# Attention with a recurrent state: TensorE's instructions in slots of a fixed order

## The chip, the cores and the metric

The kernel runs on one core of a Trainium2 chip. The time is that of the device for one execution, in microseconds, as the median of several runs. The engines are TensorE (PE, with its weight loads PEld), VectorE (DVE), ScalarE (ACT), GpSimd (POOL) and SyncE (SP, whose queue issues nearly all DMAs). Each engine takes its instructions strictly in the order in which the compiler queued them.

## The reference

Attention keeps a 40 x 40 state for each of 4 x 8 heads and walks 768 steps; a mixture of eight experts follows, of which every token takes two.

```python
for t in range(S):                                    # S = 768, state [B, H, 40, 40]
    y[:, :, t] = np.einsum('bhd,bhde->bhe', rt, state)
    Sa = np.einsum('bhde,bhe->bhd', state, at)
    state_decay = state * wt[:, :, None, :] - np.einsum('bhd,bhe->bhde', Sa, bt)
    state = state_decay + np.einsum('bhd,bhe->bhde', vt, kt)
x = y.transpose(0, 2, 1, 3).reshape(B * S, H * D)      # 3072 x 320
logits = x @ w_gate
noisy_logits = logits + np.log1p(np.exp(x @ w_noise)) * noise
# the two best of 8 experts per token, softmax over the two, then
out[mask] += top2_w[mask, k, None] * (np.maximum(x[mask] @ w1[e], 0.0) @ w2[e])
```

## The kernel before, in words

*Units.* The 768 steps are cut into 12 chunks of 64, the four batches into two pairs p. A unit n is one chunk of one pair (24 units, n = 2 cc + p), with 8 heads x 2 batches in it. Four units in a row (two chunks of both pairs) make a group g of six.

*Preparation of a group.* `prepA` loads w, b and a, takes running products of w (DVE), logarithm and exponential (ACT), products (DVE, POOL), splits b and a into two 16-bit halves (`pack`), sends them through DRAM and loads them back as `st_ab` in the layout for TensorE (five such buffers, `SAB=5`). `scoresL` multiplies b with a for each chunk and copies the result into `lt` and `lo`, which go through DRAM into the tile X; `tsolve` inverts the triangular 32 x 32 blocks of X in 60 instructions, on DVE for group 0 and on POOL for the others (L552, L553); the result returns through DRAM (`fetchB`) as `dT`, one buffer for each pair. `prepC` does for k what `prepA` does for b and a.

*A unit.* `pre` multiplies k with a (`psc`, masked to `ak`) and starts W with ak times v. `chain` adds the state times a to W, splits W into two halves (`split320`, L609 on ACT and L610 on DVE), applies dT to get Q (`apply`, 24 matmuls), copies it (L646), corrects the lower half of W by it, splits again, applies dT again to get U, copies U three times (L653 to L655) and forms the next state S of its pair. `state` splits the state and stacks it, `turned` transposes it. `outp` transposes U, forms scores with r for both batches (`psc`, masked to P, L676), sums the output Y, and multiplies it by the gate `pgm` into xt (L687). `blocks` transposes k and b into `kb`. `logits` stores xt, transposes it and multiplies by the gate's weights; after tiles 8, 16, 20, 22 and 24 `route` picks the experts, counts places with matmuls (`pr`, L137 to L140) and leaves indirect DMAs on POOL that scatter the entries (L162), which are held back until the last `tsolve` is issued.

*Order.* A scheduler at compile time queues each engine's instructions by a simulated time, by priority where several are ready: the chain is raised by `PRIO`. `burst` chains the matmuls of one tile, so that they stay together; between bursts the scheduler is free. `ND=(2,0,0,0)` puts two matmuls without use ahead of Q (`warm`). The loop over units is in `run` (L721 to L741): `prepA` of a later group is issued `LA=7` units ahead, `prepC` `LC=4`, `fetchA` and `fetchB` two units ahead. PSUM has eight banks: one `psc`, one `pst`, three `pacc` (W, Q, U, S, Y), two `pt`, one `pp`.

*After attention* `experts` loads the weights of each expert, gathers its rows and multiplies; it isn't touched.

Of the kernel before, what the change touches and what calls it, by code (L numbers as in the profile page):

```python
# [21 lines left out]
NA=20  # L22
# [3 lines left out]
SG=1  # L26
# [15 lines left out]
class Moe:  # L42
    def __init__(s,nc,tc,ctx,aps):
        s.nc,s.tc=nc,tc
        s.wgn_d,s.nz_d,s.w1_d,s.w2_d,s.out_d=aps
        ec=ctx.enter_context
        s.kp=ec(tc.tile_pool(name="mk",bufs=1))
        s.rp=ec(tc.tile_pool(name="mr",bufs=MRB))
        s.dp=ec(tc.tile_pool(name="md",bufs=1,space=DRAM))
        s.scat=[]; s.half=0; s.parts=PARTS; s.cap=CAP; s.rts=list(RTS); s.todo=[]; s.sg=None  # L50
        s.consts()
# [50 lines left out]
    def logits(s,n,xt,ps,tag,bufs=(1,1)):  # L102

        nc=s.nc
        s.xw=nc.sync.dma_start(s.xd[n>=NA][128*n:128*n+128],xt)
        px=ps.tile([128,3,128],F32,name="px",tag=tag[0],bufs=bufs[0])
# [3 lines left out]
        pl=ps.tile([128,16],F32,name="pl",tag=tag[1],bufs=bufs[1])  # L110
# [16 lines left out]
    def route(s,n0,T,ps,tag,bufs):  # L127
# [7 lines left out]
        cnt=r("cnt",dt=F16); nc.vector.tensor_tensor(cnt,oh[:,:,0],oh[:,:,1],op=ALU.add)  # L135
        pr=ps.tile([128,T,8],F32,name="pr",tag=tag,bufs=bufs)
        nc.tensor.matmul(pr,s.tri,cnt,start=True,stop=False,skip_group_check=True)  # L137
        nc.tensor.matmul(pr,s.ones,s.cumh.rearrange("p (o e)->p o e",o=1).to_broadcast([128,T,8]),start=False,stop=False,skip_group_check=True)
        for j in range(T-1):
            nc.tensor.matmul(pr[:,j+1:],s.ones,cnt[:,j:j+1].to_broadcast([128,T-1-j,8]),start=False,stop=j==T-2,skip_group_check=True)  # L140
# [244 lines left out]
class Att:  # L385
    PSC=1; PACC=3; PT=2; PPB=1
    def __init__(s,nc,tc,ctx,aps):
# [9 lines left out]
        s.psa=ec(tc.tile_pool(name="psa",bufs=1,space=PSUM)); s.psb=ec(tc.tile_pool(name="psb",bufs=1,space=PSUM)); s.ps=ec(tc.tile_pool(name="ps",bufs=1,space=PSUM))  # L397
        s.consts()
    def consts(s):
# [7 lines left out]
        m=s.wk.tile([128,128],F32,name="mfull",tag="ak"); nc.gpsimd.memset(m,IS)  # L407
# [17 lines left out]
        s.tri=t([128,32,32],F16,name="tri"); nc.gpsimd.memset(s.tri,1.0)  # L425
        nc.gpsimd.affine_select(out=s.tri,in_=s.tri,pattern=[[-1,32],[1,32]],base=0,channel_multiplier=0,compare_op=ALU.is_gt,fill=0.0)
# [41 lines left out]
    def prepA(s,p,g):  # L468
# [26 lines left out]
        gm=s.tmp.tile([120,2,3,CG],F32,name="gm")  # L495
# [35 lines left out]
    def scoresL(s,G,gi,scr):  # L531

        nc=s.nc
        lt=s.tmp.tile([128,CG,8,32],F32,name="lt",bufs=LTB)
        lo=s.tmp.tile([128,CG,8,32],F32,name="lo",bufs=LOB)
        for c in range(CG):
            pp=s.score64(G['b'][c],G['a'][c],"pp",s.PPB)
            for z,t0 in ((lt,0),(lo,32)): nc.scalar.activation(z[:,c],pp[:,:,t0:t0+32],AF.Copy,scale=-(2.0**-18))
        for i in range(4):
            s.sl=s.nc.sync.dma_start(scr[gi,i].rearrange("c h (j t)->j (c h) t",j=32),(lt,lo)[i%2][32*i:32*i+32].rearrange("p c h t->p (c h) t"))  # L540
        G['lo']=lo
    def tsolve(s,scr,eng):
# [3 lines left out]
        eng.tensor_tensor(Xt,Xt,s.tri,op=ALU.mult)  # L546
# [8 lines left out]
        nc.scalar.activation(th[...,0],Xt,AF.Copy,scale=SC)  # L555
        nc.vector.scalar_tensor_tensor(th[...,1],Xt,SC,th[...,0],op0=ALU.mult,op1=ALU.subtract)
# [4 lines left out]
    def fetchA(s,G,cc,c,n):  # L561
        nc=s.nc; o={'n':n,'G':G,'c':c}; p=G['p']
# [6 lines left out]
        rv=s.RV[n%2]  # L569
        for j in range(2): nc.sync.dma_start(rv[64*j:64*j+48,j:j+2].rearrange("p x i b t->p (x i b t)"),s.aps[3][p,cc,j])  # L570
# [8 lines left out]
    def warm(s,src,k):  # L579
        if not k: return  # L580
        for _ in range(k): s.nc.tensor.matmul(src,s.idh,s.dm[:,0:320],start=True,stop=True)
# [107 lines left out]
    def run(s,m,xo=None):  # L689
# [3 lines left out]
        def prepA(g,p):  # L693
            if p==0: grp[g]=[]; scr[g]=s.dr.tile([2,4,CG,8,1024],F32,name="scr")
# [198 lines left out]
```

## Time and profile before

| what | us |
|---|---|
| three runs | 1025.58, 1022.32, 1024.23 |
| median | 1024.23 |
| the profiled execution | 1027.86 |
| its span, first to last instruction | 1026.1 |
| busy in the span: PE, PEld | 793.2, 704.1 |
| busy: DVE, ACT, POOL | 512.5, 397.6, 475.2 |

The span has four parts: preparation of the first group until 99 us, attention until about 580, the change-over to the experts until 606, and the experts. A row of a group of instructions names the line, engine, operation, tile written and tiles read, shapes and number; then busy us, mean ns of one, and the idle time of the engine just before with what ended it. A row in order of time begins with its start in us and its duration.

### The profile page before, as it was taken

The numbers are of one execution on the slowest core, as the hardware profiler recorded it, in microseconds if no ns is written. First come the engines' busy times: TensorE is split into PE (matmuls) and PEld (weight loads), VectorE is DVE, ScalarE is ACT, GpSimd is POOL, SyncE is SP. The second block draws the span as 40 slices with busy tenths as digits, with TensorE's granted clock in tenths as the row PEclk, the third lists the DMA queues.
The fourth block names the chain that finished last, engine by engine and source line by source line (L and its number), as shares of the span: only waits on it lengthen the run. The fifth ranks groups of instructions, "written<-read, shape, count | busy, mean of one in ns | idle before, by whom it ended". The sixth has DMA issues, their size and how long they took to land.

```text
span 1026.1 us, 25154 instructions
## 1 busy us (share of the span) xinstructions
PE 793.2 (77%) x10506; PEld 704.1 (69%) x10506; DVE 512.5 (50%) x1023; ACT 397.6 (39%) x816; POOL 475.2 (46%) x616
## 2 busy tenths in 40 slices
PE   0111557729687787998799569999999999999995
PEld 0111446518575676877688449999999989999995
DVE  9359874443566446447355542644344434443430
ACT  2202343423353344455454322544344434343421
POOL 6201347968347818827875235133333333333313
PEclk9999975868687677899899669999999999999998
DMA  3794998393579358666265753526252525252303
GB/s 96 190 202 125 231 247 216 87 257 100 141 195 249 95 125 204 160 142 179 76 129 138 241 166 61 136 49 149 49 149 49 148 50 147 51 147 51 36 7 39
DMA packets 135264, 136.20 MB, mean 133 GB/s; under 512 B 67393, under 2 KB 114949, under 8 KB 135061
## 3 DMA queue, kind: packets, MB, share of 16 engines
q1 hardware_dynamic: 123492, 117.35, 43.1%
q0 software_dynamic: 11648, 17.15, 9.5%
q8 instruction: 85, 1.39, 0.6%
q14 instruction: 39, 0.31, 0.1%
HBM read 96.48 MB, written 41.37 MB: 134 GB/s over the span
## 4 chain that ended last, share of the span: by engine, by line
PE 46%; POOL 16%; DMA 14%; DVE 10%; issue 8%; ACT 3%; SPq 2%; POOLq 0%; ACTq 0%; DVEq 0%
PE po L295 16%; PE ph L273 13%; POOL X L553 6%; POOL Tt L552 5%; PE pY L452 3%; DMA X<-scr 3%; PE psc L452 2%; PE pW L452 2%; PE pt L254 2%; DMA d_ab<-pk 2%; DMA rawk<-in_fm_dram 2%; DMA out_dram<-y,le 2%; DMA xr<-xd,le 1%; PE pQ L452 1%; POOL X L546 1%
## 5 line engine op out<-in xcount | busy, mean ns | idle before, releaser
L297 POOL DMA_INDIRECT out_dram<-y,le x56 | 92.5, 1652 | 201.3 <-ACT y L296 172.1
L276 DVE SCALAR_TENSOR_TENSOR hl<-ph,hh 128x256 fp32r<-128x256 f32 (+1 forms) x128 | 71.0, 557 | 154.7 <-ACT hh L274 154.3
L274 ACT ACTIVATE hh<-ph 128x320 fp32r<-128x320 f32 (+1 forms) x128 | 66.2, 519 | 156.6 <-PE ph L273 156.5
L553 POOL TENSOR_TENSOR X<-X,Tt 128x30 f32<-128x30 f32 (+9 forms) x150 | 86.6, 577 | 10.6
L241 POOL DMA_INDIRECT xr<-xd,le x56 | 54.3, 970 | 74.3 <-DMA le<-ls 33.0
L552 POOL TENSOR_TENSOR Tt<-X 128x30 f32<-128x30 f32 (+9 forms) x150 | 82.0, 547 | 10.0
L295 PE MATMUL po<-w2h,hh 128*128 128x320 f32 x384 | 74.6, 314 | 0.0
L273 PE MATMUL ph<-xh,w1h 128*128 128x512 f32 (+1 forms) x256 | 71.3, 362 | 0.5 <-ACT xh L257 0.5
L273 PE MATMUL ph<-xh,w1l 128*128 128x512 f32 (+1 forms) x256 | 69.7, 354 | 0.0
L273 PE MATMUL ph<-xl,w1h 128*128 128x512 f32 (+1 forms) x256 | 69.0, 351 | 0.0
L295 PE MATMUL po<-w2l,hh 128*128 128x320 f32 x384 | 68.3, 312 | 0.0
L295 PE MATMUL po<-w2h,hl 128*128 128x320 f32 x384 | 68.1, 309 | 0.0
L452 PEld LDWEIGHTS <-st_ab 120*64 120x64 f16 (+1 forms) x928 | 28.6, 123 | 51.7 <-issue 41.8
L295 PEld LDWEIGHTS po<-w2h,hh 128*128 128x128 f32 x384 | 61.3, 188 | 3.1
L452 PE MATMUL psc<-RV,uT 128*64 128x128 f32 x384 | 59.9, 306 | 4.2 <-DVE P L676 3.9
L676 DVE TENSOR_TENSOR P<-psc,mk 128x512 f32<-128x512 f32 x48 | 33.0, 688 | 56.2 <-PE psc L452 55.8
L452 PEld LDWEIGHTS <-dT 128*128 128x128 f16 x1152 | 39.8, 102 | 29.4 <-issue 14.8
L452 PE MATMUL psc<-RV 128*64 128x128 f32 x384 | 60.0, 306 | 0.0
L295 PEld LDWEIGHTS po<-w2h,hl 128*128 128x128 f32 x384 | 59.3, 188 | 0.1
L295 PEld LDWEIGHTS po<-w2l,hh 128*128 128x128 f32 x384 | 58.9, 188 | 0.4
L452 PE MATMUL pQ<-w,dT 128*128 128x40 f16 x1152 | 42.1, 187 | 21.6 <-DMA dT<-scr 10.0
L162 POOL DMA_INDIRECT ls<-ent,po x48 | 47.4, 988 | 19.3 <-issue 14.1
(299 smaller groups left out, 1939.2 us busy)
## 6 DMA issues: line engine op xcount, KB each, us to landing
w2r<-in_w_dram SPq DMA_DIRECT2D x8, 1280.0 KB
RV<-in_rv_dram SPq DMA_DIRECT2D x48, 192.0 KB
rawba<-in_fm_dram SPq DMA_DIRECT2D x24, 360.0 KB
d_ab<-pk SPq DMA_DIRECT2D x24, 360.0 KB
st_ab<-d_ab SPq DMA_DIRECT2D x36, 240.0 KB
w1r<-in_w_dram SPq DMA_DIRECT2D x8, 1024.0 KB
raww<-in_fm_dram SPq DMA_DIRECT2D x12, 365.6 KB
st_ab<-d_ab SPq DMA_DIRECT2D x24, 180.0 KB
```

The source lines that it names most:

```text
L162: st=nc.gpsimd.indirect_dma_start(out=s.ls[s.half],out_offset=OFFS(ap=po[:,j,k:k+1],axis=0),in_=s.ent[:,j,k],in_offset=None)
L241: for k in range(c,c+a): nc.gpsimd.indirect_dma_start(out=x[:p,k],out_offset=None,in_=s.xd[w],in_offset=OFFS(ap=li[:p,k,0:1],axis=0))
L254: for t,p in tiles(t0,n): nc.tensor.transpose(pt[:,t-t0:t-t0+p],x[:p,t//128,f0:f0+128],s.idm[:p,:p])
L273: for i,(a,b) in enumerate(mm): nc.tensor.matmul(ph[:,:n],a,b,start=i==0,stop=i==7)
L274: nc.scalar.activation(hh[:,f,:n],ph[:,:n],AF.Relu)
L276: if c.stop>c.start: nc.vector.scalar_tensor_tensor(o,ph[:,c],0.0,hh[:,f,c].bitcast(F32),op0=ALU.max,op1=ALU.subtract)
L295: nc.tensor.matmul(po[:p],h[:,f,r],w[:,f],start=k==0,stop=k==23); k+=1
L297: st=nc.gpsimd.indirect_dma_start(out=s.out_d,out_offset=OFFS(ap=idx[:p,ii],axis=0),in_=y[:p],in_offset=None,compute_op=ALU.add)
L452: def mm(s,*a,**k): return lambda: s.nc.tensor.matmul(*a,**k)
L552: eng.tensor_tensor(t,Xt[:,j:j+1,j+1:].to_broadcast([128,j,m]),Xt[:,0:j,j:j+1].to_broadcast([128,j,m]),op=ALU.mult)
L553: s.tl=eng.tensor_tensor(Xt[:,0:j,j+1:],Xt[:,0:j,j+1:],t,op=ALU.add)
L676: nc.vector.tensor_tensor(m,pp.rearrange("p i j t->p (i j) t"),s.mk.to_broadcast([128,8,64]),op=ALU.mult)
```

## The change

`burst` now chains each matmul or transpose of attention to the one before it in the program, whatever tile it is of, and the route's matmuls go through it too: PE's order is the order in which the program is written. `chain`, `pre` and `outp` are cut into steps, and `slot(n)` writes them out: unit n's chain with steps of the output of n-1, of the keys and the state of n+1, of the logits of n-2, and of the scores of a group in between. Two more buffers for the turned state, one more for kb; ak has one. `psc` has two banks, which the state's stacking and the group scores share. `route` is cut in two, its matmuls come a slot later. X is masked by a select instead of a product, and the constant for it is gone. The matmuls without use are gone. `LA` is 8, the loads of r and v (`fetchR`) are issued after those of k and v of the next but one unit.

```diff
-            s.route(s.n0,s.rts.pop(0),ps,tag[1],bufs[1])
+        if j==s.rts[0]-1: s.pend=s.route1(s.n0,s.rts.pop(0)); s.n0=n+1
+    def places(s,ps,tag,bufs):
+        if s.pend is None: return
+        n0,T=s.pend[:2]; n=n0+T-1
+        s.route2(*s.pend,ps,tag,bufs); s.pend=None
...
     def burst(s,f):
-        last=None
         for g in f:
-            with (s.tc.high_priority(offset=BURST) if last is not None else ExitStack()): i=g()
-            if last is not None: s.tc.add_manual_dep(i.ins,last.ins.name,...)
-            last=i
+            i=g()
+            if s.pel is not None: s.tc.add_manual_dep(i.ins,s.pel.ins.name,...)
+            s.pel=i
...
-    PSC=1; PACC=3; PT=2; PPB=1
+    PSC=2; PACC=3; PT=2; PPB=1
...
-            pp=s.score64(G['b'][c],G['a'][c],"pp",s.PPB)
+        pp=s.score64(G['b'][c],G['a'][c],"psc",s.PSC)
...
-        eng.tensor_tensor(Xt,Xt,s.tri,op=ALU.mult)
+        nc.gpsimd.affine_select(out=Xt,in_=Xt,pattern=[[-1,32],[1,32]],base=0,channel_multiplier=0,compare_op=ALU.is_gt,fill=0.0)
...
-        nc.scalar.activation(th[...,0],Xt,AF.Copy,scale=SC)
-        nc.vector.scalar_tensor_tensor(th[...,1],Xt,SC,th[...,0],op0=ALU.mult,op1=ALU.subtract)
+        for r in (slice(0,16),slice(16,32)):
+            nc.scalar.activation(th[:,r,:,0],Xt[:,r],AF.Copy,scale=SC)
+            nc.vector.scalar_tensor_tensor(th[:,r,:,1],Xt[:,r],SC,th[:,r,:,0],op0=ALU.mult,op1=ALU.subtract)
...
-            pe=s.psa.tile([120,8,40],F32,name="pst",tag="pst",bufs=1)
+            pe=s.psa.tile([120,8,40],F32,name="pst",tag="psc",bufs=s.PSC)
...
-        sD=s.wk.tile([128,4,2,40],F32,name="sD",bufs=1)
+        sD=s.wk.tile([128,4,2,40],F32,name="sD",bufs=3)
...
+    def slot(s,n,O,x,m,sc):
+        o,oP,oN=O.get(n),O.get(n-1),O.get(n+1)
+        if o:
+            if not first: s.burst([s.mm(W[...],o['a'](h,b),o['sE'][:,b,h],...) for h,b in HB()])
+            w1=s.split320("w1",W,IS)
+        if oP: s.scores(oP,0)
+        if sc: s.scoresL(*sc,0)
+        if n-2 in x: x[n-2]['xT']=m.turned(x[n-2]['xt'],s.ps,"pt",s.PT)
+        if sc: s.scoresL(*sc,1)
+        if o:
+            Q=...; s.apply(Q,dT,pr(w1,0),pr(w1,1),True,True)
+            q=...; nc.scalar.activation(q,Q,AF.Copy)
+        if oN:
+            s.keys(oN)
+            if oN['cc']: oN['sD']=s.turned(oN['G']['p'])
+        if o:
+            s.burst([s.mm(W[...],o['lo'][r(b),h],q[r(b),h],...) for h,b in HB()])
+            w2=s.split320("w1",W,IS)
+        if oP: s.scores(oP,1); s.gates(oP)
+        if o:
+            U=...; s.apply(U,dT,pr(w2,0),pr(w2,1),True,True)
+            (three copies of U as before)
+        if oN and oN['cc']: oN['sE']=s.estack(oN['G']['p'])
+        m.places(s.ps,"pp",s.PPB)
+        if n-2 in x: m.logits(n-2,x[n-2]['xT'],s.ps,"pp",s.PPB)
+        if o and not last:
+            (S as before, from the split state and U, into Sst)
+            s.split(p)
+        if o: s.uturned(o)
+        if oN: s.blocks(oN)
+        if oP:
+            s.outp(oP); x[n-1]={'xt':oP['xt'][:,0:DM]}
+            m.put(n-1,x[n-1]['xt'])
+        if sc: s.gamma(sc[0])
+        if oN: s.sums(oN)
...
+        sc={1:(1,0),2:(1,1)}
+        for g in range(2,NG): n=max(4*g-LS,3); sc[n]=(g,0); sc[n+1]=(g,1)
+        for n in range(N+3):
+            ga,qa=divmod(n+LA,4); gc,qc=divmod(n+LC,4)
...
+            with s.tc.high_priority(offset=PRIO): s.slot(n,O,x,m,L)
+            if L and p:
+                prepT(g)
+                if g==NG-1: m.sg=s.tl.ins
+            if 1<ga<NG and qa<2: prepA(ga,qa)
+            if 0<gc<NG and qc<2: s.prepC(grp[gc][qc])
+            fB(n+2); fA(n+2)
+            if 0<n<N-1: s.fetchR(O[n+1])
...
-LA=7; LC=4; RB=3
+LA=8; LC=4; RB=3; LS=6
...
-ND=(2,0,0,0)
-KBB=2
+KBB=3
```

More of the change, by code (lines that the diff above doesn't have):

```diff
@@ L135, in route, with route2 @@
         cnt=r("cnt",dt=F16); nc.vector.tensor_tensor(cnt,oh[:,:,0],oh[:,:,1],op=ALU.add)
+        return n0,T,oh,cnt
+    def route2(s,n0,T,oh,cnt,ps,tag,bufs):
+        nc=s.nc; mm=lambda *a,**k: (lambda: nc.tensor.matmul(*a,**k,skip_group_check=True))
+        r=lambda name,sh=(8,),dt=F32: s.rp.tile([128,RT,*sh],dt,name=name)[:,0:T]
         pr=ps.tile([128,T,8],F32,name="pr",tag=tag,bufs=bufs)
[L137 to L140, printed above, removed]
+        s.burst([mm(pr,s.tri,cnt,start=True,stop=False),mm(pr,s.ones,s.cumh.rearrange("p (o e)->p o e",o=1).to_broadcast([128,T,8]),start=False,stop=False)]
+                +[mm(pr[:,j+1:],s.ones,cnt[:,j:j+1].to_broadcast([128,T-1-j,8]),start=False,stop=j==T-2) for j in range(T-1)])
         h=s.rp.tile([128,8],F16,name="cumh",bufs=len(RTS)); p=s.cumh
@@ new lines, in scores, with gates @@
+    def scores(s,o,b):
+        nc=s.nc
+        pp=s.psa.tile([128,4,2,64],F32,name="psc",tag="psc",bufs=s.PSC)
+        s.burst([s.mm(pp[64*j:64*j+64,i],x[:,i,b],o['rr'][:,:,i,b],start=True,stop=True) for i in range(4) for j,x in ((1,o['uT']),(0,o['v']))])
+        m=s.wk.tile([128,8,64],F32,name="P",bufs=2)
+        nc.vector.tensor_tensor(m,pp.rearrange("p i j t->p (i j) t"),s.mk.to_broadcast([128,8,64]),op=ALU.mult)
+        o['P'].append(m)
+    def gates(s,o):
+        nc=s.nc; xt=o['xt']=s.wk.tile([128,360],F32,name="xt",bufs=2)
+        pg=s.ps.tile([128,360],F32,name="pgm",tag="pp",bufs=s.PPB)
+        s.burst([s.tp(pg[:,120*hh:120*hh+120],o['ng'][:,hh],s.idf[:120,:120]) for hh in range(3)])
+        nc.scalar.activation(xt.rearrange("p (a g e)->p a g e",a=3,g=3),pg.rearrange("p (a e g)->p a g e",a=3,g=3),AF.Copy,scale=-(2.0**-12))
@@ L682, in outp, with run, score @@
         s.burst([s.mm(Y[64*b:64*b+64,HS[h]],P[b][:,h],kb[:,b,h],start=sD is None and h==0,stop=True,skip_group_check=True) for h,b in HB(1)])
[L683 to L689 removed]
+        xt=o['xt'][:,0:DM]
+        nc.vector.tensor_tensor(xt,Y.rearrange("p h e->p (h e)"),xt,op=ALU.mult)
+    def run(s,m):
         nc=s.nc
[L691 removed]
+        grp={}; scr={}; scr2={}; O={}; x={}; s.sfs={}
         N=NG*4
         def prepA(g,p):
[L694 to L696 removed]
+            if p==0: grp[g]=[]
+            grp[g].append(s.prepA(p,g))
+        def score(g,p):
+            if p==0: scr[g]=s.dr.tile([2,4,CG,8,1024],F32,name="scr")
+            for c in range(CG): s.scoresL(grp[g][p],p,scr[g],c)
+            s.gamma(grp[g][p])
         def prepT(g):
@@ L710, in run @@
         gate=(s.sd0,s.sl)
         s.prepC(grp[0][0],gate)
[L712 removed]
+        with after(s.sl.ins): fA(0); s.fetchR(O[0])
         s.prepC(grp[0][1],gate)
[L714 to L719 removed]
@@ L742 @@
-LA=7; LC=4; RB=3
+        with after(s.sl.ins): fA(1); s.fetchR(O[1])
+        s.keys(O[0]); s.blocks(O[0]); s.sums(O[0]); fB(0); fB(1)
+        with after(xd): prepA(1,0); prepA(1,1)
+        with after(xd),(ExitStack() if 0 in MG else after(pl)): m.consts2(s.dm.bitcast(F32))
+        sc={1:(1,0),2:(1,1)}
+        for g in range(2,NG): n=max(4*g-LS,3); sc[n]=(g,0); sc[n+1]=(g,1)
+        for n in range(N+3):
+            ga,qa=divmod(n+LA,4); gc,qc=divmod(n+LC,4)
+            L=None
+            if n in sc:
+                g,p=sc[n]
+                if p==0: scr[g]=s.dr.tile([2,4,CG,8,1024],F32,name="scr")
+                L=grp[g][p],p,scr[g]
+            with s.tc.high_priority(offset=PRIO): s.slot(n,O,x,m,L)
[6 more added lines that the diff above has]
+            if 0<n<N-1: s.fetchR(O[n+1])
+            if ZN<n<=ZN+4:
+                with after(m.xw.ins): m.zero(n-1-ZN)
```

200 lines of the change are left out of this document (71 added, 129 removed).

## The prediction

> **What bounds the kernel now.** I read the page's slices first, then the busy time by stage, then single rows for where the units stand, and last who waits for whom. The slices show four stages.
>
> ```profile
> PE   0111557729687787998799569999999999999995
> DVE  9359874443566446447355542644344434443430
> POOL 6201347968347818827875235133333333333313
> PEclk9999975868687677899899669999999999999998
> ```
>
> The same by stretches; behind the times stand busy us (and instructions) of PE, PEld, DVE, ACT and POOL, then granted clock, DMA share and GB/s:
>
> ```profile
> 99.00:231.00 132.00, 73.25 (x1354) 62.41 (x1355) 78.43 (x101) 50.49 (x106) 79.87 (x96) 0.76 0.80 206
> 231.00:426.00 195.00, 157.15 (x3184) 133.82 (x3182) 106.31 (x194) 84.73 (x190) 122.53 (x176) 0.75 0.61 157
> 426.00:519.00 93.00, 81.59 (x2038) 69.98 (x2033) 48.72 (x121) 44.96 (x112) 60.67 (x113) 0.96 0.56 140
> 519.00:561.00 42.00, 40.80 (x998) 35.02 (x999) 23.89 (x78) 21.39 (x57) 29.03 (x35) 1.00 0.52 116
> 561.00:606.00 45.00, 25.07 (x295) 19.14 (x291) 22.96 (x88) 14.44 (x31) 14.86 (x18) 0.61 0.77 246
> 606.00:1026.00 420.00, 404.90 (x2454) 374.74 (x2453) 164.12 (x311) 161.46 (x293) 141.24 (x107) 0.99 0.36 82
> ```
>
> The experts, from 606 on, are PE's own time (404.9 of 420 us busy) and are not touched. What can move lies between 99 and 606, in the 24 units of attention. The rows of ACT's copy of Q mark units 0, 4, 20 and 23:
>
> ```profile
> 99.17 0.42 ACT L646 ACTIVATE q<-pQ 128x320 f32<-128x320 f32 x1
> 231.32 0.44 ACT L646 ACTIVATE q<-pQ 128x320 f32<-128x320 f32 x1 [5.05 <-PE pQ L452]
> 522.20 0.44 ACT L646 ACTIVATE q<-pQ 128x320 f32<-128x320 f32 x1 [1.19 <-PE pQ L452]
> 560.67 0.44 ACT L646 ACTIVATE q<-pQ 128x320 f32<-128x320 f32 x1 [0.63 <-PE pQ L452]
> ```
>
> Units 4 to 20 take (522.20-231.32)/16 = 18.2 us each, units 20 to 23 only (560.67-522.20)/3 = 12.8 us. The work per unit is the same; the last ones have no group to prepare and the full clock, the middle ones have PE busy for 157 of 195 us at a mean clock of 0.75. So in the middle TensorE is neither starved nor full: it does its work slowly and loses some 38 us in gaps. What it waits for from 100 to 575 us:
>
> ```profile
> PE px L107 <- DVE xt L687: 22.1, 10, 7.2
> PE psc L452 <- ACT lo L538: 12.5, 4, 5.9
> PE pQ L452 <- DMA dT<-scr: 10.0, 1, 10.0
> PE psc L452 <- DMA st_ab<-d_ab: 8.6, 2, 6.4
> ```
>
> Total, number, longest. The first two are waits of order: the turned x of the unit just finished stands at the head of PE's queue before its output is made, and the second group score waits for the only buffer it shares. The third is unit 4 alone, where group 1's triangular solve is late. That solve is GpSimd's. The chain of work that ended last has the starts for groups 1 to 5 (five rows, start and us), the order of time on ACT its first copy out of groups 1 and 5 (two rows):
>
> ```profile
> 149.62 2.14 POOL X L546
> 223.65 2.13 POOL X L546
> 299.94 2.85 POOL X L546
> 389.99 2.65 POOL X L546
> 465.62 2.15 POOL X L546
> 209.60 1.33 ACT L555 ACTIVATE th<-X 128x1024 f16<-128x1024 f32 x1 [3.48 <-POOL X L553]
> 503.53 1.34 ACT L555 ACTIVATE th<-X 128x1024 f16<-128x1024 f32 x1 [6.71 <-POOL X L553]
> ```
>
> Undisturbed (group 5) it takes 503.53-465.62 = 37.9 us; group 1's takes 60.0, since other work of GpSimd stands between its steps. Solves start 74 to 90 us apart, so from group 2 on GpSimd has slack and the solve isn't what holds the units.
>
> **The change, part by part.** *Order on TensorE.* Every PE instruction of attention is now chained to the one before, in slots: unit n's chain (W, Q, q, W, U, S), with the output scores of n-1, keys and turned state of n+1 and x of n-2 in the places where the chain waits for ACT and DVE. The wait for xt (22.1 us) goes, because x is turned two slots later, and that for lo (12.5 us), because group scores use a ring of two. What is late next: the chain itself needs no filler that isn't a slot old, so the next is PE's own work. That work per unit at full clock is 40.80/42 of 12.82 us = 12.45 us. The two filling matmuls per unit go:
>
> ```profile
> L581 PE MATMUL pQ<-dm,idh 128*128 128x320 f16 x48 | 13.9, 382 | 0.0
> ```
>
> 13.9/24 = 0.58 us, of which they also covered the wait for the split of W; the output scores of n-1 now cover that. Floor: 12.45-0.58 = 11.9 us; I take 12.4 for units without preparation, nearest to the 12.8 measured, as a hand-made order will leave some gaps.
>
> *Group scores and routing.* The scores of groups 1 and 2 stand in slots 1 to 4, those of a later group g in slots 4g-6 and 4g-5, and a slot's Q is queued behind them. The second one needs a load into a buffer that is freed only in slot 4g-6 (five st_ab buffers). One such load, from the chain of work that ended last:
>
> ```profile
> 159.10 10.73 DMA st_ab<-d_ab
> ```
>
> 10.7 us, plus some us of queue, against one slot: hidden if slots are 14 us, with a stall of 0 to 5 us per group otherwise; all of PE stands still then. I put it at 2 us per group, inside the pace below. Routing's matmuls move one slot behind the gates: hidden, since GpSimd's scatter stays behind the last solve.
>
> *GpSimd.* With units faster, the solves become the next limit. Its rows:
>
> ```profile
> L553 POOL TENSOR_TENSOR X<-X,Tt 128x30 f32<-128x30 f32 (+9 forms) x150 | 86.6, 577 | 10.6
> L552 POOL TENSOR_TENSOR Tt<-X 128x30 f32<-128x30 f32 (+9 forms) x150 | 82.0, 547 | 10.0
> L526 POOL TENSOR_TENSOR rawk<-rawk,NH 120x384 f32<-120x384 f32 x20 | 21.9, 1113 | 19.6 <-DMA rawk<-in_fm_dram 19.6
> L500 POOL TENSOR_TENSOR rawba<-rawba,NH 120x768 f32<-120x768 f32 x8 | 14.5, 1811 | 21.6 <-DVE NH L486 13.2 <-DVE pk L442 5.0 <-DVE nge L493 2.2
> L502 POOL TENSOR_TENSOR rawba<-rawba,NG__4044 120x768 f32<-120x768 f32 x1 | 3.3, 3345 | 0.1
> L488 POOL TENSOR_TENSOR NG__4044<-Gx,raww 120x768 f32<-120x768 f32 x1 | 1.5, 1494 | 15.2 <-PE pgm L453 15.2
> ```
>
> Per group: solve 37.9 us; preparation 4 x 1.11 + 2 x 1.81 + 2 x 2.6 (between 1.8 and 3.3) + 2 x 1.5 = 16.3 us. The mask of X becomes a select instead of a product with a constant:
>
> ```profile
> L546 POOL TENSOR_TENSOR X<-X,tri 128x1024 f32<-128x1024 f32 x5 | 11.9, 2373 | 35.6 <-DMA X<-scr 35.6
> L426 POOL TENSOR_SCALAR_AFFINE_SELECT tri<-tri 128x1024 f16<-128x1024 f16 x1 | 1.3, 1256 | 0.0
> ```
>
> 2.37 us against 1.26 us of the same size in 16-bit: between +0.1 (if 32-bit takes twice as long) and -1.1 us per group; I take -0.5, too little for the sum. Cutting the last copy of the solve into halves lets DVE start half of ACT's 1.3 us earlier; also below 1 us.
>
> So the cycle of a group is 54.2 us (13.6 per unit) where all waits of GpSimd are filled with preparation, and 54.2 + 35.6/5 = 61.3 us (15.3 per unit) where each load of X is waited for as now. TensorE (12.4) is below both, DVE far below: 106.31 us in the 195 us row are 106.31/(195/18.2) = 9.9 us per unit. I take 14.5 us per unit, the middle of the two, and put the stalls on group scores into it. The ends: 12.9, if preparation runs ahead and only TensorE counts, and 18.2, no change.
>
> *The clock* decides whether 14.5 can be had. Busy PE, granted clock, DMA share and GB/s in three stretches:
>
> ```profile
> 325.60:329.00 3.40, 3.28 (x84) 1.00 0.68 245
> 329.00:332.40 3.40, 2.02 (x58) 1.00 1.04 246
> 335.80:349.50 13.70, 12.03 (x157) 0.50 0.11 34
> ```
>
> After 3.4 us in which PE was busy for 59% the clock was halved, and it stayed so for many us with PE nearly always busy: slow work doesn't leave gaps enough to see. With 12.4 us of work in a 14.5 us slot PE is busy for 85%, in the 426 to 519 us stretch it was 81.59/93 = 88% at a clock of 0.96. I therefore reckon with nearly full clock.
>
> The Trainium skill, "TensorE: Matmul & The Clock Gate", Part 1, says that the clock is halved after an idle window of about 3.4 us. The row at 329 us disagrees: that window was 59% busy, so a slot that is merely half idle is enough. By the page's rule an order without long gaps would always keep the full clock, and the time would be that of the second rival below. The same page's section on a second failure mode, cycling through PSUM buffers, says that short idles between groups of matmuls make the clock oscillate; this speaks against the change, whose scores, keys and turned state share a ring of two, and by it the third rival holds.
>
> *Start to unit 4's Q.* Group 1's scores stand in slots 1 and 2, its second st_ab load came late already, so X starts at 149.6 as before. Preparation of group 2 and keys of group 1 are issued ahead of the solve, one unit earlier, instead of between its steps. Lower end 37.9 us for the solve, upper end 60.0; I take 46. From its end to unit 4's copy of Q went 231.32-209.60 = 21.7 us, kept. Unit 4: 149.6+46+21.7 = 217.3, a gain of 14 (ends: 22 and 0). Slots 0 to 3 are done by then.
>
> *Queues.* The loads of r and v move from two units ahead to behind the other loads of a slot. SP's queue, which is in order, stood for them:
>
> ```profile
> SPq L570 <- PE psc L452: 19.7, 14, 3.5
> ```
>
> 19.7 us in 14 waits, with dT and st_k loads behind; the new place is after the last reader, so that wait goes; if it doesn't (GpSimd or DVE late), 19.7/14 = 1.4 us per unit, still hidden by the slot between load and use. dT of n+2 is issued when slot n ends, with more than a slot to go. *Buffers:* the state is turned one slot before it was and is read two slots later, hence three buffers; ak falls to one, which keys and sums of a slot use in turn. kb has three as it lives one slot longer. No cost, as its cover is a slot's 12 us.
>
> *Tail.* From unit 23's Q to the experts were 606-560.67 = 45.3 us, with PE busy for 25.07 of 45. The last x is now turned in slot 25 and its places found in slot 26, both almost empty: +2 us (ends: -5, if w1's load comes sooner, and +10).
>
> **Sum.** Unit 4: -14. Sixteen units: 16 x 14.5 = 232 against 290.9, -59. Last three steps: 3 x 12.4 = 37.2 against 38.5, -1. Tail: +2. Together -72: the span of 1026.1 becomes 954. The profiled execution took 1027.86, the median of the runs is 1024.23 (3.6 less), so 952 us is the forecast. Differences under 0.3% (3 us) are what a measurement of this kernel can't tell from no change.
>
> **The rivals.** *Full clock throughout (chance 0.20).* Preparation fills every gap of GpSimd, and units run at 12.9 from unit 4 on: -22 - (290.9-206.4) - 1 + 2 = -105, so 919 (900 to 930). For it: units 20 to 23 do this already. Against: 54.2 us of GpSimd per group.
>
> *The clock stays low (0.22).* The fixed order waits now on one, now on another engine in each slot, DVE's long preparation steps above all, and PE stays cold half of the time. Pace 16.8, half-way between 15.3 and 18.2: -7 - (290.9-268.8) - 1 + 4 = -26, 998 (975 to 1020). For it: the mean clock of 0.75 in both stretches; against: px and lo, the largest waits, are gone.
>
> *Slower (0.08).* The second group score stands ahead of Q, and its load can't start before slot 4g-6. If the load lands so late that TensorE stands still 20 us per group, then four groups take 4 x (58+20) = 312 against 290.9, and with -14, -1 and +2 as before the time is about 1032; it decides from 72.7-58 = 14.7 us of stall per group on, some 18 with unit 4's gain. Against: 10.73 us for that load. For: buffers that PE frees late do hold preparation up, as the 15.2 us in the row of NG show.
>
> *Nothing (0.05).* Starts of X stay 74 us apart, now because preparation comes later by as much as TensorE comes sooner, and the units wait for their solves: 4 x 72.7 = 290.9 again, 1024.
>
> Forecast 0.45 (930 to 975). Faster: 0.45 + 0.20 + 0.21 of the third; same 0.05; slower 0.09 with the third's rest. From 903 to 1004 lie all of the first, most of the second and three quarters of the third, 0.8 in all.
>
> **What would show it.** Copies of Q: unit 4 at about 217, 20 at 449, 23 at 487; experts at 534. Granted clock above 0.9 from unit 5 on; no wait of px for xt and of psc for lo; GpSimd's starts of X about 58 us apart. Wrong would be: Q of unit 4 still at 231; psc waiting for st_ab over 5 us in each group (fourth case); starts of X at 74 or more with clock 0.75 (third); or solves that wait for scores while PE is full at 12.9 (second).

## The result, and the profile after

The changed kernel takes 1063.32 us (median of four runs, 1060.90 to 1064.99); the kernel before takes 1024.90 us in four runs beside it. The ratio is 1.037 (95% interval 1.032 to 1.041): slower by 3.7%, where 952 us had been forecast. The profiled execution took 1062.72 us with a span of 1061.0.

Two rows of the slices of the changed kernel's page, as shown of the kernel before:

```profile
PE   0112576237965575699489828999999999999995
PEclk9999988557867696689799959999999999999998
```

In slices 11 to 16 (counted from 0; some 290 to 450 us, in the middle of attention) PE is busy for 5 to 7 tenths, where it was 7 to 9 before; the clock there is at 6 to 9, where it was 6 to 8. The experts, from slice 24 on, look the same. The rows of ACT's copy of Q, in order of time, mark units 4, 20 and 23 of the changed kernel:

```profile
230.82 0.44 ACT L656 ACTIVATE q<-pQ 128x320 f32<-128x320 f32 x1 [10.79 <-PE pQ L459]
557.87 0.44 ACT L656 ACTIVATE q<-pQ 128x320 f32<-128x320 f32 x1 [0.17 <-PE pQ L459]
596.18 0.44 ACT L656 ACTIVATE q<-pQ 128x320 f32<-128x320 f32 x1 [0.17 <-PE pQ L459]
```

With the spans this places the whole loss. Unit 4 comes 0.5 us earlier (230.82 against 231.32). The 16 units from 4 to 20 take 327.05 us instead of 290.88, so +36.2, or 20.4 us each. Units 20 to 23 take 38.31 instead of 38.47. From unit 23 to the end it is 1061.0-596.18 = 464.8 instead of 465.4. Together +34.9 us, and 1061.0-1026.1 is 34.9. Only the middle units lost.

One row for that stretch, first of the kernel before, with the columns of the windows in the prediction:

```profile
231.30:522.20 290.90, 241.66 (x5268) 206.32 (x5268) 156.11 (x317) 130.59 (x303) 185.57 (x289) 0.82 0.59 151
```

and of the changed one:

```profile
230.80:557.90 327.10, 239.18 (x5378) 214.92 (x5380) 159.94 (x330) 135.58 (x321) 207.62 (x299) 0.80 0.56 144
```

PE's busy time and clock hardly differ (241.66 at 0.82, 239.18 at 0.80). Its idle time does: 290.90-241.66 = 49.2 us before, 327.10-239.18 = 87.9 after. So the time was lost in waits of TensorE. What they are for between units 4 and 20 (total, number, longest), first three lines of the kernel before, where ptr waits for no uT at all:

```profile
PE psc L452 <- ACT lo L538: 11.2, 3, 5.9
PE px L107 <- DVE xt L687: 9.7, 4, 5.8
PE pS L452 <- DVE vu L654: 3.8, 3, 3.2
```

and the four largest of the changed one:

```profile
PE ptr L459 <- DVE uT L463: 23.1, 12, 9.1
PE pS L459 <- DVE vu L669: 17.4, 5, 7.9
PE px L108 <- DVE xf L203: 14.8, 1, 14.8
PE psc L459 <- DVE P L699: 7.2, 2, 7.1
```

Of the two waits that the change was to take away, psc for lo is gone, and px for xt is down to 1.1 us in one wait. But these four, 62.5 of the 87.9 us, all name DVE, an engine that is busy for 159.94 of 327.10 us. So the next question is what DVE waits for there. The largest row, the second half of each split of W, is a step of the chain itself and was 25.9 us before; the next are xt and steps of preparation:

```profile
DVE w L616 <- ACT w L615: 35.3, 25, 2.4
DVE NH L490 <- POOL rawk L533: 23.6, 4, 7.4
DVE xt L713 <- PE pY L459: 23.4, 11, 3.6
DVE pk L450 <- ACT pk L449: 16.2, 8, 5.3
DVE th L565 <- ACT th L564: 13.8, 3, 12.3
DVE Gx L484 <- POOL NG__3846 L495: 7.7, 1, 7.7
DVE Gx L484 <- POOL NG__5366 L495: 6.6, 1, 6.6
```

Lines of the same view of the kernel before have the last of these waits at 0.6 us each and xt behind pY at 1.8; NH waits for no rawk in it:

```profile
DVE w L610 <- ACT w L609: 25.9, 21, 6.3
DVE th L556 <- ACT th L555: 16.6, 4, 7.2
DVE pk L442 <- ACT pk L441: 9.7, 4, 4.0
...
DVE xt L687 <- PE pY L452: 1.8, 5, 0.4
...
DVE Gx L477 <- POOL NG__4044 L488: 0.6, 1, 0.6
DVE Gx L477 <- POOL NG__5487 L488: 0.6, 1, 0.6
```

It had that wait only ahead of unit 4, where two of them are in its view from 100 to 575 us:

```profile
DVE NH L483 <- POOL rawk L526: 9.4, 2, 5.0
```

The chain of work that ended last shows one wait for rawk as a whole (start, us, what), in the changed kernel:

```profile
314.87 7.71 DMA rawk<-in_fm_dram
...
322.71 1.95 POOL rawk L533 x2
324.69 1.34 DVE NH L490
...
326.06 0.51 DVE vu L669
```

And DVE's own order at that time:

```profile
316.62 0.69 DVE L699 TENSOR_TENSOR P<-psc,mk 128x512 f32<-128x512 f32 x1
324.69 1.34 DVE L490 TENSOR_TENSOR NH<-Gx,raww 120x768 f32<-120x768 f32 x1 [7.38 <-POOL rawk L533]
326.06 0.50 DVE L669 TENSOR_SCALAR vu<-pQ 64x320 f32<-64x320 f32 x1
```

NH is a product of `prepA` for the next group, into one of two buffers. The older contents of that buffer are still read by GpSimd's product of `prepC` (rawk, L533), which waits for a load that landed at 322.6. NH stands at the head of DVE's queue for 7.38 us, and vu, a step of the unit's chain, stands behind it. TensorE's next instruction in its fixed order needs vu, and so TensorE stands as well. With `LA=8` and `LC=4`, `prepA` of group g+1 and `prepC` of group g are issued in the same pass of the loop, `prepA` first; with `LA=7` it came a pass later.

The third of TensorE's four waits, 14.8 us at once, has another step at the head of DVE's queue: th, DVE's part of splitting the last solve's result, stood there 12.33 us for ACT's part. The xt that px turns came behind it and ended at 527.95 us. The profile puts the wait down to xf, which ended at 528.03. So px still waited for xt once, and longer than before (two rows of DVE, one of PE):

```profile
525.61 0.73 DVE L565 SCALAR_TENSOR_TENSOR th<-X,th 128x512 f16<-128x512 f32 x1 [12.33 <-ACT th L564]
527.47 0.48 DVE L713 TENSOR_TENSOR xt<-pY,xt 128x320 f32<-128x320 f32 x1
528.09 0.87 PE L108 MATMUL px<-idm,xt 128*128 128x128 f32 x3 [14.81 <-DVE xf L203]
```

### The profile page after: what moved, and what is told of

Its sections match the earlier page's. It is cut to its first block, busy times and chain, and to the rows that moved or that the text cites. A ratio compares the mean times of both kernels' runs of the same rounds, so it can differ in the third digit from the quotient of the medians.

```text
span 1061.0 us, 25084 instructions
## 1 busy us (share of the span) xinstructions
PE 770.1 (73%) x10458; PEld 699.6 (66%) x10458; DVE 504.2 (48%) x1028; ACT 396.8 (37%) x822; POOL 477.1 (45%) x615
## 4 chain that ended last, share of the span: by engine, by line
PE 48%; DMA 20%; DVE 12%; POOL 10%; issue 5%; SPq 3%; ACT 2%; POOLq 0%; DVEq 0%; ACTq 0%
PE po L304 16%; PE ph L282 14%; DMA rawk<-in_fm_dram 6%; PE pY L459 3%; PE psc L459 3%; POOL X L561 3%; POOL Tt L560 3%; PE pW L459 3%; DMA rawba<-in_fm_dram 2%; DMA d_ab<-pk 2%; PE pt L263 2%; PE pQ L459 2%; DMA le<-ls 1%; POOL rawk L533 1%; DMA xr<-xd,le 1%
## 5 line engine op out<-in xcount | busy, mean ns | idle before, releaser
L561 POOL TENSOR_TENSOR X<-X,Tt 128x30 f32<-128x30 f32 (+9 forms) x150 | 93.6, 624 | 11.0
L560 POOL TENSOR_TENSOR Tt<-X 128x30 f32<-128x30 f32 (+9 forms) x150 | 84.9, 566 | 10.5
L459 PE MATMUL psc<-RV,uT 128*64 128x128 f32 x384 | 64.3, 321 | 3.2 <-DVE uT L463 2.8
L459 PE MATMUL psc<-RV 128*64 128x128 f32 x384 | 64.6, 321 | 0.2 <-issue 0.2
L554 POOL TENSOR_SCALAR_AFFINE_SELECT X<-X 128x1024 f32<-128x1024 f32 x6 | 7.8, 1292 | 109.0 <-DMA X<-scr 109.0
```

Of the source, the lines that this page charges most:

```text
L459: def mm(s,*a,**k): return lambda: s.nc.tensor.matmul(*a,**k)
L560: eng.tensor_tensor(t,Xt[:,j:j+1,j+1:].to_broadcast([128,j,m]),Xt[:,0:j,j:j+1].to_broadcast([128,j,m]),op=ALU.mult)
L561: s.tl=eng.tensor_tensor(Xt[:,0:j,j+1:],Xt[:,0:j,j+1:],t,op=ALU.add)
```

## The experiments

The kernel before took 1021 to 1025 us on two of the chips, and about 1074 us on two others (see the last section), so kernels are compared by their ratio to the kernel before on the same chip. The microseconds in the expectations are for a kernel before of about 1024 us. The theory: DVE's queue, held by preparation at its head, stops a TensorE whose order is fixed. The rivals: the fixed order costs by itself, whatever DVE does; the earlier start of the preparation costs by itself, in any order; the clock costs it, since gaps let it fall.

**a_cfirst: prepC ahead of prepA in a pass.**

```diff
-            if 1<ga<NG and qa<2: prepA(ga,qa)
             if 0<gc<NG and qc<2: s.prepC(grp[gc][qc])
+            if 1<ga<NG and qa<2: prepA(ga,qa)
```

> The changed kernel with one swap: in the loop over units, k of a group is prepared ahead of w, b and a of the next group. Theory Q (VectorE's queue): preparation steps that wait for GpSimd stand in VectorE's queue ahead of the chain, and TensorE, whose order is fixed, stands still behind them. The wait of NH for rawk (23.6 us from 231 to 470) comes from a buffer of NH that the product of k of the group before still holds; the swap takes most of it away: 1035 to 1050 us, wait of NH for rawk under 10 us. Theory O (the order itself: TensorE can't go round whatever is late): another thing is late instead, 1055 to 1066 us.

1033.99 us, ratio 1.010 (1.006 to 1.015), so 2.7 points of the 3.7 were this order. Units 4 to 20 took 300.9 us. NH's wait for rawk is gone from DVE's waits, as the theory had it. TensorE's wait for uT and DVE's for pY, which stand beside it, have stayed:

```profile
PE ptr L459 <- DVE uT L463: 16.6, 14, 4.5
```

```profile
DVE xt L713 <- PE pY L459: 21.9, 10, 3.7
```

**b_la8: the kernel before, with LA=8 alone.**

```diff
-LA=7; LC=4; RB=3
+LA=8; LC=4; RB=3
```

> The kernel before with LA=8 alone, so that w, b and a of a group are prepared one unit earlier, with TensorE's order left free. Theory Q: VectorE waits for GpSimd as in the changed kernel, some of it covered by the free order: 1035 to 1055 us. Theory O: no harm without the fixed order, 1018 to 1030 us.

1063.95 us, ratio 1.037 (1.030 to 1.043): this one number, in the old order, costs as much as the whole change did, more than either theory had expected. DVE's waits there show the same row, which between units 4 and 20 the kernel before doesn't have:

```profile
DVE NH L483 <- POOL rawk L526: 14.4, 4, 4.9
```

**a_free: the changed kernel, with TensorE's order left to the scheduler** (`burst` as before, so that only the matmuls of one tile are chained).

```diff
-            i=g()
-            if s.pel is not None: s.tc.add_manual_dep(i.ins,s.pel.ins.name,...)
-            s.pel=i
+            with (s.tc.high_priority(offset=BURST) if last is not None else ExitStack()): i=g()
+            if last is not None: s.tc.add_manual_dep(i.ins,last.ins.name,...)
+            last=i
```

> The changed kernel with the chaining of the kernel before: only the matmuls of one tile are kept together, and the scheduler orders the rest of TensorE. Slots, buffers, LA=8 and the order of issue stay. Theory Q: VectorE's queue holds the same preparation, the loss stays: 1050 to 1075 us. Theory O: the loss is gone, 1000 to 1030 us.

1020.87 us, ratio 0.997 (0.994 to 0.999): the time that theory O had expected. The wait on DVE that theory Q names is still there in full,

```profile
DVE NH L491 <- POOL rawk L534: 24.2, 4, 10.8
```

and yet units 4 to 20 took 271.7 us (239.8 to 511.5). So the same wait costs far less where the scheduler orders TensorE than where the order is written out: neither theory is right alone. The scheduler queues the other engines by the same simulated time, so their orders differ too; that TensorE's order alone makes the difference is likely, not shown.

**a_dve: all products of preparation on DVE, none on GpSimd.**

```diff
-MD=(0,1); MG=(); MK=(0,); TG=0
+MD=(0,1,2,3,4,5); MG=(1,2,3,4,5); MK=(0,1,2,3,4,5); TG=0
```

> The changed kernel with all products of preparation on VectorE (NG, b, a and k of all groups), so that GpSimd has the solves alone and VectorE waits for none of its products. VectorE gets about 2.4 us more per unit. Theory Q: the waits of NH and of Gx for GpSimd are gone, and the solve of a group takes 38 to 45 us: 985 to 1020 us. Theory O: VectorE, with more to do, is late more often: 1050 to 1080 us.

1035.25 us, ratio 1.011 (1.007 to 1.015), a miss: 985 to 1020 was expected. GpSimd is out of the way, but the load that it had waited for is now waited for by DVE itself:

```profile
DVE rawk L533 <- DMA rawk<-in_fm_dram: 34.5, 6, 10.6
```

So freeing DVE of GpSimd isn't enough: DVE stands at its head for the load instead. That this is what kept the time up is argued from this one row. This is also the kernel in which unit 4 came earliest (215.2).

**a_la7: the changed kernel with the old LA=7.**

```diff
-LA=8; LC=4; RB=3; LS=6
+LA=7; LC=4; RB=3; LS=6
```

> The changed kernel with LA=7 as in the kernel before; slots, buffers and TensorE's fixed order stay. Theory L (the lead of preparation over k's preparation is the loss, since NH's buffers are then held by k's product): as with the swap, 1025 to 1045 us. Theory O (fixed order): the loss stays, 1050 to 1070 us.

1079.45 us, ratio 1.006 (1.004 to 1.007): `LA` is a second cure, as good as the swap (3.1 points). It leaves a rest: even without `LA=8` the change costs 0.6 points, where the forecast for the whole had been a gain of 7.

**a_lc6: prepC two units earlier instead.**

```diff
-        with after(xd): prepA(1,0); prepA(1,1)
+        with after(xd): prepA(1,0); prepA(1,1); s.prepC(grp[1][0]); s.prepC(grp[1][1])
-            if 0<gc<NG and qc<2: s.prepC(grp[gc][qc])
+            if 1<gc<NG and qc<2: s.prepC(grp[gc][qc])
-LA=8; LC=4; RB=3; LS=6
+LA=8; LC=6; RB=3; LS=6
```

> The changed kernel with LC=6, so that k of a group is prepared two units earlier and well ahead of the next group's w, b and a. Theory L: no wait of NH for rawk, and k's load, now early, holds nobody: 1015 to 1035 us. Theory O: 1045 to 1066 us.

1092.05 us, ratio 1.017 (1.011 to 1.022), a miss: the wait of NH for rawk is gone as expected, but only 2.0 points came back, and two waits of Gx for NG (7.2 and 5.1 us) remained. What else the earlier prepC displaced isn't settled.

**f_cfirst: order left to the scheduler, and prepC first.**

> Both at once: the free chaining of the kernel before and the swap of k's preparation ahead of the next group's. If the two losses are the same one (fixed order only passes on VectorE's waits), the swap has nothing left to win: 1015 to 1025 us. If they add up, 985 to 1005 us.

1054.20 us, ratio 0.983 (0.978 to 0.988), 1.4 points better than a_free. So the two losses add up at least in part: the swap helps in the free order too, by half as much as in the fixed one (2.7).

**a_warm: 24 matmuls without use ahead of S in units 4 to 15 of the changed kernel,** to keep TensorE from idling.

```diff
+            if 3<n<16: s.burst([s.mm(Sp,s.idh,s.dm,start=True,stop=True)]*24)
```

> The changed kernel with 24 matmuls without use ahead of S in units 4 to 15, where TensorE waits for VectorE's copy of U; in the units without such a wait they cost some 3 us each at full clock. Theory C (the low clock multiplies the waits): the halved clock between Q of unit 4 and of unit 20 falls from 134 us to under 90 and the time to 1045 to 1060 us in spite of the added work. If the clock matters little: 1080 to 1100 us.

1135.86 us, ratio 1.058 (1.054 to 1.061). Units 4 to 12 of this kernel as one row,

```profile
231.10:426.60 195.50, 146.72 (x2931) 125.58 (x2931) 90.25 (x178) 74.93 (x171) 114.30 (x162) 0.84 0.55 143
```

and the same units of the changed one:

```profile
230.80:412.00 181.20, 129.68 (x2735) 116.37 (x2737) 91.65 (x178) 74.34 (x171) 111.26 (x158) 0.75 0.58 153
```

The granted clock rose from 0.75 to 0.84, and the stretch got 14.3 us longer; PE's idle time was 48.8 us instead of 51.5, though other waits now lead it (ptr for kb, 16.7 us). So a higher clock that is bought with added work didn't pay here. That the clock isn't what lost the time rests on the rows of units 4 to 20 in the section on the result: TensorE is busy for about as long, at 0.82 before and 0.80 after.

**b_la8c: the kernel before with LA=8 and prepC first.**

> The kernel before with LA=8 and the swap (k of a group prepared ahead of the next group's w, b and a), TensorE's order free. Theory L (a lead over k's preparation is what hurts, whatever TensorE's order): the 3.7% that LA=8 cost it are gone, ratio to before 0.99 to 1.01. If the longer lead itself hurts (buffers, transfers): 1.025 to 1.04.

1041.83 us, ratio 1.021 (1.016 to 1.025). Of the 3.7 points 1.6 are the order in the pass, and NH's wait for rawk is gone with them; the other 2.1 are the lead itself, in the old order. Which wait that is was not separated; the second group score's wait for st_ab, 10.0 us in three waits between units 4 and 20, is one candidate (the kernel before has none there).

The rest of a_cfirst, ptr waiting for uT and xt for pY, pointed at `blocks`. The slot has `uturned`, `blocks`, `outp` in a row. `uturned` and the two halves of `blocks` (ptr from k and from b) share a ring of two PSUM buffers, so the third needs the first copied out by DVE. The changed kernel, PE in order of time:

```profile
450.72 1.12 PE L460 MATMUL pu<-idf,Ut 128*128 128x128 f32 x4
451.63 0.47 PE L459 MATMUL ptr<-cmb,st_k 120*128 120x40 f16 x8
452.62 0.42 PE L459 MATMUL ptr<-cmb,st_ab 120*128 120x40 f16 x8 [0.52 <-DVE uT L463]
452.97 1.94 PE L459 MATMUL pY<-sD,RV 128*64 128x40 f32 x32
```

and DVE at that time:

```profile
450.84 0.49 DVE L680 SCALAR_TENSOR_TENSOR Sst<-pS,gam 128x320 f32<-128x320 f32 x1 [1.39 <-PE pS L459]
451.87 0.69 DVE L463 COPY uT<-pu 128x512 f32<-128x512 f32 x1 [0.55 <-PE pu L460]
```

The output pY, which depends on none of this, stands behind ptr, and xt on DVE then waits for pY: two queues that hold each other up, here for 0.52 us. Without NH's wait, in a_cfirst, the 14 such waits shown there come to 16.6 us.

**a_blk: prepC first, and blocks behind outp; the order stays fixed.**

```diff
         if o: s.uturned(o)
-        if oN: s.blocks(oN)
         if oP:
             s.outp(oP); x[n-1]={'xt':oP['xt'][:,0:DM]}
             m.put(n-1,x[n-1]['xt'])
+        if oN: s.blocks(oN)
         if sc: s.gamma(sc[0])
```

> The changed kernel with the swap, and in each slot the turned blocks of k and b moved behind the output sums, in the fixed order. With the swap alone TensorE waited some 1.2 us per unit at the blocks for VectorE's copy of the turned U, whose buffer they need. Theory O2 (the fixed order loses at places of its own, one after another): 1.2 us of 14 units and some clock, ratio to before 0.985 to 1.0 where the swap alone gave 1.010. If the wait only moves to the next place: 1.005 to 1.015.

992.18 us, ratio 0.973 (0.968 to 0.978): faster than both kernels, 3.7 points below a_cfirst. Units 4 to 20, then 20 to 23:

```profile
229.30:489.80 260.50, 225.03 (x5383) 198.27 (x5384) 159.49 (x329) 134.79 (x320) 191.48 (x296) 0.89 0.70 177
489.80:525.50 35.70, 34.65 (x906) 30.98 (x906) 21.43 (x68) 20.02 (x52) 20.37 (x26) 1.00 0.58 138
```

Of the 66.6 us that the first stretch lost against the changed kernel, 87.9-35.5 = 52.4 are idle time of PE and 14.2 are the same matmuls at a higher clock (0.89 against 0.80). A unit takes 16.3 us, and 11.9 without preparation. One wait of ptr for uT is left, 2.5 us. That of xt, 23.4 us between units 4 and 20 of the changed kernel, is here between units 4 and 23:

```profile
DVE xt L713 <- PE pY L459: 7.1, 8, 1.3
```

**a_blk0: the blocks moved, prepA still first.**

> The changed kernel with the turned blocks moved behind the output sums, without the swap. If the two causes are independent (swap 0.027, blocks 0.037 of the time before): ratio to before 0.995 to 1.005. If the move also lets VectorE get past the late products, so that the swap is worth little: 0.97 to 0.985. If the swap is needed first: over 1.02.

1074.30 us, ratio 1.001 (0.999 to 1.002). The swap is worth 2.7 points with (1.001 to 0.973) and without (1.037 to 1.010) the move, the move 3.7 and 3.6 with and without the swap: two causes that add. NH's wait for rawk is there in full (23.3 us in four waits).

**f_blk: the free order with both.**

> Swap and moved blocks with TensorE's order left to the scheduler. If the fixed order's only loss was the place of the blocks, the scheduler, which chose its own place, has nothing to win: 0.975 to 0.99, as with swap and free order (0.983), the fixed order now better by some 0.01. If the fixed order still loses elsewhere: 0.95 to 0.97.

1061.47 us, ratio 0.987 (0.983 to 0.990), no better than f_cfirst: a free order needn't be told where the blocks go. With both flaws gone the fixed order is ahead of it: 0.973 in a_blk, and on the same chip as this kernel 0.978 in a_blknd (below). It isn't ahead in the middle units, though. Of the 10.9 us between f_blk's span and a_blknd's, unit 4's Q gives 13.1 (239.9 against 226.8) and the part from unit 23 to the end 5.4, while units 4 to 23 take 7.7 us more in the fixed order. Why unit 4 comes later in the free order wasn't separated; ACT's copy of group 1's solve starts at 227.9 us there and at 214.5 in a_blknd.

**a_blknd: a_blk with two matmuls without use ahead of each Q,** as the kernel before had them.

```diff
+            s.burst([s.mm(Q,s.idh,s.dm,start=True,stop=True)]*2)
             s.apply(Q,dT,pr(w1,0),pr(w1,1),True,True)
```

> Swap and moved blocks in the fixed order, with two matmuls without use ahead of each Q, as in the kernel before. By the forecast's term (0.58 us per unit, on the path where TensorE is the limit): 24 x 0.58 = 14 us at most, ratio 0.977 to 0.987 against 0.973. If TensorE waits there anyway: 0.97 to 0.976.

1051.66 us, ratio 0.978 (0.975 to 0.982): 0.5 points above a_blk, some 5 us, with intervals that overlap. The most that the filling could cost by the forecast's term was 14 us.

**a_blkth and f_th: the split of the solve's result (th) on GpSimd instead of ACT and DVE,** in a_blk and in f_cfirst, to take another preparation step out of DVE's queue.

Group 0, solved on DVE, keeps the old lines; the branch for it is left out below.

```diff
-            nc.scalar.activation(th[:,r,:,0],Xt[:,r],AF.Copy,scale=SC)
-            nc.vector.scalar_tensor_tensor(th[:,r,:,1],Xt[:,r],SC,th[:,r,:,0],op0=ALU.mult,op1=ALU.subtract)
...
+            nc.gpsimd.tensor_scalar(Xt[:,r],Xt[:,r],SC,None,op0=ALU.mult)
+            nc.gpsimd.tensor_copy(th[:,r,:,0],Xt[:,r])
+            nc.gpsimd.tensor_tensor(th[:,r,:,1],Xt[:,r],th[:,r,:,0],op=ALU.subtract)
```

> As the kernel with the moved blocks, and the solve's halves are made on GpSimd right behind the solve, so that neither ScalarE nor VectorE stands at its head waiting for a solve. TensorE waited 10 to 15 us for that once, at the last solve, and VectorE 18 us in all. GpSimd gets some 7 us more per group. Theory Q (a queue's head that waits for GpSimd is what the fixed order pays for): another 0.01 to 0.02 lower than with the moved blocks. If GpSimd's solves are the limit by now: the same or 0.01 higher.

> Free order within the slots, the swap, and the solve's halves on GpSimd. Free order and swap alone gave 0.983. Theory Q: VectorE's wait for solves (15 us) is gone, 0.965 to 0.98. If the free order had covered that wait already: 0.98 to 0.99.

1042.19 us, ratio 1.019 (1.016 to 1.022), and 1044.98 us, ratio 1.023 (1.020 to 1.027): both far slower, and beyond what either theory had expected. The solves now are what TensorE waits for, in a_blkth

```profile
PE pQ L459 <- DMA dT<-scr: 85.3, 4, 46.4
```

The longest, 46.4 us, ends at unit 4. Such a wait is there in other kernels too (10.0 us in the kernel before, 35.8 in the changed one, 43.5 in a_blk). The other three, 38.9 us together, are between units 4 and 20, where a_blk has no wait for dT. GpSimd has no room for more work in its solves.

**a_blkg2: a_blk, with the preparation of group 2 and the keys of group 1 on DVE,** to free GpSimd for group 1's solve.

```diff
-MD=(0,1); MG=(); MK=(0,); TG=0
+MD=(0,1,2); MG=(2,); MK=(0,1); TG=0
```

> Swap and moved blocks in the fixed order, and the products of group 2's preparation (NG, b, a) and of group 1's k on VectorE instead of GpSimd, so that the first solve on GpSimd, which took 63 to 67 us with them between its steps, has GpSimd nearly alone. If that work holds unit 4: first solve 45 us or less, Q of unit 4 at 205 to 215 us instead of 229, ratio 0.955 to 0.968. If VectorE, now with that work, holds the units 0 to 3 and the scores by as much: Q of unit 4 at 225 or later, 0.97 to 0.985.

1047.79 us, ratio 0.978 (0.973 to 0.983): no gain, the second case of the expectation. Q of unit 4 came at 230.2 us; other products of preparation stand between the steps of the solve (160.2 to 217.9 us) in place of those that were moved, 11.9 us of them against 11.6 in a_blk.

**The same stretch in all of them.** Ratios from different chips are comparable only if a slow chip adds about the same to every kernel. Units 4 to 12 can be compared without that, as they lie ahead of the stretch in which TensorE stands still on those chips (last section). From ACT's copies of Q, in us:

| kernel | order on TensorE | unit 4's Q | units 4 to 12 | ratio |
|---|---|---|---|---|
| before | free | 231.3 | 159.9 | 1 |
| b_la8 | free | 232.5 | 188.7 | 1.037 |
| b_la8c | free | 222.2 | 179.8 | 1.021 |
| changed | fixed | 230.8 | 181.2 | 1.037 |
| a_cfirst | fixed | 226.6 | 170.9 | 1.010 |
| a_blk0 | fixed | 236.2 | 148.5 | 1.001 |
| a_blk | fixed | 229.3 | 140.7 | 0.973 |
| a_blknd | fixed | 226.8 | 143.6 | 0.978 |
| a_free | free | 239.8 | 146.2 | 0.997 |
| f_cfirst | free | 238.9 | 135.4 | 0.983 |
| f_blk | free | 239.9 | 138.7 | 0.987 |

The swap takes 8 to 11 us off these eight units in either order, and the move of the blocks 30 to 33 in the fixed one: the two causes add here too. The free order with the swap has the shortest of these stretches, but reaches unit 4 some 10 us later.

## Why the prediction was wrong

*The step that failed* is in "Order on TensorE": "the chain itself needs no filler that isn't a slot old, so the next is PE's own work", and with it "DVE far below" at 9.9 us per unit. DVE's load was right (159.94/16 = 10.0 us per unit) and answers the wrong question. A unit's chain passes through DVE in both splits of W, in the copy vu of U and in the new state, and DVE takes its work in order, so its price is how long the instruction at its head waits, not how much it has to do. The sum took 14.5 us per middle unit (-59) from GpSimd's cycle and put DVE's waits at nothing; it was 20.4 (+36), beyond the forecast's upper end of 18.2. Two details made it: NH behind rawk, undone by the swap (2.7 points, some 27 us), and ptr behind uT, undone by the move of the blocks (3.7 points, some 37 us). With both gone the middle units took 16.3 us and the time was 992, which is the forecast's mechanism at half its size: 260.5 against 290.9 is -30, where -59 was forecast. That leaves 40 us to the forecast, 16 x 1.8 = 29 of them here and 12 at unit 4. What holds these units 1.8 us above 14.5 stays open; TensorE is idle for 35.5 us there, in many small waits, the largest line of which is 7.0 us.

*LA=8* was read as a gain ("one unit earlier") and priced for unit 4 alone. What stood in the diff was that `prepA` of one group and `prepC` of the group before it now share a pass, with `prepA` first and two buffers for NH between them. In the kernel before, this number by itself cost 3.7%.

*The rival that came nearest* was "the clock stays low": "the fixed order waits now on one, now on another engine in each slot, DVE's long preparation steps above all". The mechanism is the one found; its sign was not: it was taken at 16.8 us per unit, between the bound of GpSimd and no change. The waits of DVE were given no price above the old pace, though the old view had NH waiting for rawk already (9.4 us). Its sign showed in part: the selects of X, the first step of a solve, start 69 to 98 us apart (156.5, 225.2, 298.1, 396.1, 488.0), with the clock at 0.80. The rival that ended slower had a wait for st_ab as its mechanism; between units 4 and 20 the changed kernel has no such wait.

*Unit 4*: -14 was forecast, -0.5 came. All three terms were off. The solve's first step on GpSimd starts at 156.5 us, not 149.6, and its result is copied at 218.6, so it takes 62.2 us, not 46; from there to unit 4's Q it is 12.2 us, not 21.7. Between the steps of the solve stand products of preparation for 11.8 us and two waits for their loads for 5.6; without them it would be 44.8. In a_dve, where GpSimd has no such products, the solve takes 48.4 us (154.4 to 202.8), and unit 4 came at 215.2. So the step that failed here is that preparation would be ahead of the solve; it still stood between its steps.

*The clock* was expected above 0.9 as PE would be busy for 85% of a slot. It was 0.80 at 73% busy, and 0.89 at 86% (225.03/260.50) in a_blk. That is near what was reckoned for a slot that is busy for 85%; it was the busy share that was wrong. The share alone doesn't set the clock: the kernel before had 0.82 at 83% (241.66/290.90). One reading on the PSUM buffers was off as well: the ring of two that scores and keys share holds the stacked state, and the turned state is in the ring of ptr and px.

*GpSimd* as the next limit didn't show in the changed kernel: it waited for loads of X instead. The select that replaced the product is right at the lower end of the forecast, 1.29 us against 2.37, -1.1 us per group. In the changed kernel's groups of instructions (its last column: idle time before, and for what):

```profile
L554 POOL TENSOR_SCALAR_AFFINE_SELECT X<-X 128x1024 f32<-128x1024 f32 x6 | 7.8, 1292 | 109.0 <-DMA X<-scr 109.0
```

Of the 109.0 us 23.3 are group 0's, which was masked on DVE before. For the same five loads GpSimd had stood idle for 35.6 us before and does so for 85.7 after. Of the kernels in slots only a_blkth and f_th, which gave it more to do, have TensorE waiting over 2 us for solves between units 4 and 20.

*Queues.* The wait of SP's queue for r and v was to go. Between units 4 and 20 it was 16.6 us in 11 waits (L570) and is 21.7 in 12 (L583). TensorE waits for no r or v there; what the loads behind it in the queue lost was not followed.

*Right* or nearly so were the units without preparation (12.4 forecast, 38.31/3 = 12.8 measured, as before, and 11.9 in a_blk), the tail (+2 forecast; from unit 23 to the end -0.6), the wait for lo that went, and the wait for xt as far as TensorE's own order made it.

## What to carry to other kernels

When an order is fixed by hand on one engine, read the other engines' queues in their order as well: for each step of the critical chain, which instruction stands ahead of it on its engine, and what the slowest thing is that this one can wait for (a buffer's last reader and the load behind that reader count). An engine that is busy for half of the time can still be what holds everything. A change of one number in a prefetch distance moves two stages past each other; write out the issue order that results, buffer by buffer, before giving it a price of nothing.

## What the runs showed of the hardware

Two of the chips ran the kernel before in about 1074 us instead of 1024. No profile of it was taken there, and no other kernel ran on chips of both kinds. In each profile of another kernel from these two chips TensorE stands still again and again in a stretch of some 40 to 50 us between 475 and 600 us, for about 1 us at a time, with nothing in the profile that it waits for; a_blk0 between 490 and 550 us:

```profile
PE pY L459 <- issue: 32.7, 26, 2.6
```

The cause wasn't sought. Matmuls without use raised the granted clock (0.75 to 0.84 in a_warm) and still made the kernel slower. And a select on GpSimd over 128 x 1024 takes as long in 32 bits (1.29 us) as in 16 (1.26 us).
